# Bounding the queries by sums of squares on ScalarE, earlier, and one feed-forward due time set to nine units

## The chip, the cores and the metric

The kernel runs on one core of one Trainium2 chip. The metric is the device time of one execution in microseconds (us). Before the change three runs took 656.70, 658.43 and 662.99 us; their median is 658.43 us. The trace shown here is of a further, profiled execution that took 653.83 us, with a span of 652.1 us on the core.

## The reference, cut to what matters

There are 4 batches, 8 heads, 576 positions and a head size of 64, all in float32.

```
scores = q @ k.T / 8 + bias[h, i, j]        # bias: a small network of log1p|i - j| / log1p(max(i, 1))
attn   = exp(scores - max); attn = attn / (sum + 1e-9)
x      = attn @ v                           # laid out as (batch, position, 512)
out    = x + relu(layernorm(x) * g @ w1) @ w2     # w1: 512 x 2048, w2: 2048 x 512
```

The kernel multiplies on TensorE partly in float32 and partly in pairs of float16 numbers (a high part and a rest). For the pairs, q, k, v and the weights are first scaled by powers of two, so that no float16 overflows. To choose these powers it needs a bound on the size of q and k in each batch. How that bound of q is worked out is what changes.

## The kernel before, in words

**Units.** The attention is cut into 144 units (a batch, a chunk of 128 query positions, a head). A loop over steps u (0 to 158) writes the program out: at step u it writes the softmax of unit u, the second half of the softmax of unit u-1, the scores of later units, the product with v of unit u-3 or u-4, and whatever is filed under that step in a table of jobs (`at(step, fn)`). A scheduler then sets the order on each engine, by priority and by its own model of times; each engine and each DMA queue afterwards runs its list in order. Chunk 4 (the 64 last positions) and chunk 0 come first, in units 0 to 47, with their scores in float32; chunks 1 to 3 are units 48 to 143, with scores in float16 pairs. Units 0 to 23 turn their probabilities round on TensorE (L621, L622) and multiply them by v in float32 (L674); later units use float16 pairs (L627, L629) that a DMA transpose on SP's queue turns round (L635, tile `pt`).

**Softmax.** L598 on VectorE adds scores and bias and takes the minimum of each row; there is one for each unit, so the n-th L598 in time marks unit n-1. L603 on ScalarE takes the exponential.

**Bounds of q and k.** For units from 48 on, `q_load` (L443 to L449) loads all queries of a batch and chunk into a tile `qb` (two DMAs of 128 KB on SP's queue, L448, each made to wait for the newest L598), and `q_abs` takes its largest absolute value for each partition into a column of `kqa`, through `absmax` (L452, a reduce on VectorE, tied to the newest L598 as well). The tiles come from a pool of two buffers (`qhp`), so a load waits until the tile two loads earlier has been read. There are 12 such tiles: loads at steps 21 to 32, reductions at steps 25 to 36. At step 43 `kq_scale` (L462 to L485) adds up the partitions with a matmul (`kqps`, L464), takes maxima (L465, L467), scales them (L469) and, one step later (`fin`, through `defer`), makes the powers of two. `split_k` (L498, L501) and `split_q` (L513, L516) use them from step 44 on for the first units in float16 pairs; L531 are those units' scores.

**Weights.** `load_w` (L791) fetches 32 pieces of the feed-forward weights on SP's queue, `decode_w` (L807, L810, L812) unpacks them on VectorE, and `split_w` (L847 on ScalarE, L850 on VectorE) makes float16 pairs. A piece is loaded into a slot only when an earlier piece is decoded.

**Feed-forward.** A finished tile of 128 rows is normalised (`ln1`, `ln2`; L734, L735 on GpSimd, L761 and L764) and then needs 8 groups of matmuls: 4 times L873 (48 matmuls, into `hps`), each followed by L879 and L883 (relu and rest) and by L902 (12 matmuls, into `y`, added up by L913). With 18 tiles there are 144 groups. They are written between the units by a bank: at each step, what the tiles that are ready still need is divided by the steps until the next tile is due (`steps_av`), and whole groups are taken out. The due time is the tile's last unit plus 8 for last units below 26, plus 10 for those from 26 to 49, plus 9 after.

Of the kernel before, what the change touches and what calls it, by code (L numbers as in the profile page):

```python
# [14 lines left out]
AF = mybir.ActivationFunctionType  # L15
ALU = mybir.AluOpType
# [6 lines left out]
def kernel(  # L23
# [13 lines left out]
    V, S, G, T, SY = nc.vector, nc.scalar, nc.gpsimd, nc.tensor, nc.sync  # L37
# [43 lines left out]
    half4 = const.tile([128, 4], F32)  # L81
    gram = {}
    kqa = const.tile([128, 28], F32)
    kqs = const.tile([128, 8], F32)
# [27 lines left out]
    def pow2(am, s, inv):  # L112
        V.tensor_scalar(out=am, in0=am, scalar1=1e-30, scalar2=1e30, op0=ALU.max, op1=ALU.min)
        V.tensor_scalar(out=s.bitcast(I32), in0=am.bitcast(I32), scalar1=EXP_BITS,
                        scalar2=EXP_BITS, op0=ALU.bitwise_and, op1=ALU.bitwise_xor)
        if inv is not None:
            V.tensor_scalar(out=inv.bitcast(I32), in0=am.bitcast(I32), scalar1=EXP_BITS,
                            scalar2=None, op0=ALU.bitwise_and)
            V.tensor_scalar(out=inv, in0=inv, scalar1=0.5, scalar2=None, op0=ALU.mult)
# [26 lines left out]
    evi, ttri = {}, {}  # L146
    vpre = {}

    def after(ins, dep):
        if dep is not None:  # L150
            tc.add_manual_dep(ins.ins, dep.ins.name,
                              mybir.DependencyInfo(mybir.DependencyClass.Sync,
                                                   mybir.DependencyReason.DATA),
                              reason="pace")
# [230 lines left out]
    def defer(fn):  # L385
        later[1].append(fn)
# [38 lines left out]
    def k_gram(n):  # L425
        b = ORD[n][0]
        early = b < 2
        ps = (ps_h if early else ps_y).tile([128, 512], F32, tag="h" if early else "y1", name="kgram")
        ops = [(g, j) for g in range(4) for j in (0, 512, 128, 256, 384)]
        for x, (g, j) in enumerate(ops):  # L430
            w = min(128, 2 * HS - j)
            kb = kt[kuse[n], g].rearrange("p a b -> p (a b)").bitcast(BF16)
            blk = kb.rearrange("p (a b) -> p a b", b=2)[:, j:j + w, 1]
            m = T.matmul(out=ps[0:w, 0:w], lhsT=blk, rhs=blk, start=(x == 0), stop=(x == len(ops) - 1))
            if x == 0:
                after(m, ttri[max(ttri)])
        am = kqa[:, 4 * b:4 * b + 1]
        V.tensor_reduce(out=am, in_=ps[:, 0:128], op=ALU.max, axis=AX.X)
        G.tensor_tensor(out=am, in0=am, in1=half4[:, 0:1], op=ALU.pow)

    qld = {}

    def q_load(b, c):  # L443
        t = qhp.tile([128, 2, 4, 128], F16, tag="qh", name="qb")
        t = t.rearrange("p x a b -> p (x a b)").bitcast(F32)
        src = q_main[b, c, 0:64].rearrange("p (e h) q -> p e (h q)", e=2)
        for e in range(2):
            after(SY.dma_start(out=t[64 * e:64 * e + 64], in_=src[:, e]), ttri[max(ttri)])  # L448
        qld[b, c] = t  # L449

    def absmax(x, col):
        red = V.tensor_reduce(out=kqa[:, col:col + 1], in_=x, op=ALU.max, axis=AX.X,  # L452
                              apply_absolute_value=True)
        after(red, ttri[max(ttri)])

    def k_abs(n, g):
        absmax(kt[kuse[n], g].rearrange("p a b -> p (a b)"), 4 * ORD[n][0] + g)

    def q_abs(b, c):
        absmax(qld.pop((b, c)), 16 + 3 * b + c - 1)  # L460

    def kq_scale():  # L462
        ps = ps_y.tile([128, 512], F32, tag="y1", name="kqps")
        T.matmul(out=ps[:, 0:28], lhsT=one_sb, rhs=kqa, start=True, stop=True)  # L464
        V.tensor_reduce(out=kqs[:, 0:4], in_=ps[:, 0:16].rearrange("p (a b) -> p a b", b=4),  # L465
                        op=ALU.max, axis=AX.X)
        V.tensor_reduce(out=kqs[:, 4:8], in_=ps[:, 16:28].rearrange("p (a b) -> p a b", b=3),  # L467
                        op=ALU.max, axis=AX.X)
        V.tensor_scalar(out=kqs, in0=kqs, scalar1=2.0 ** -13, scalar2=None, op0=ALU.mult)  # L469

        def fin():
            pow2(kqs[:, 0:4], ksc, kinv)
            V.tensor_tensor(out=kqs[:, 4:8], in0=kqs[:, 4:8], in1=kinv, op=ALU.mult)
            V.tensor_reduce(out=pmx[:, 0:1], in_=kqs[:, 4:8], op=ALU.max, axis=AX.X)
            V.tensor_scalar(out=pmx[:, 0:1], in0=pmx[:, 0:1], scalar1=2.0 ** -40, scalar2=None,
                            op0=ALU.max)
            pow2(pmx[:, 0:1], pmx[:, 1:2], pmx[:, 2:3])
            V.tensor_scalar(out=qsc, in0=kinv, scalar1=pmx[:, 1:2], scalar2=None, op0=ALU.mult)
            V.tensor_scalar(out=ipf, in0=ip_sb[:, 16:32], scalar1=pmx[:, 1:2], scalar2=None,
                            op0=ALU.mult)  # L480
            V.tensor_scalar(out=cbf, in0=cb_sb, scalar1=pmx[:, 1:2], scalar2=None, op0=ALU.mult)
            V.tensor_scalar(out=pmx[:, 2:3], in0=pmx[:, 2:3], scalar1=-0.125, scalar2=None,
                            op0=ALU.mult)

        defer(fin)  # L485

    def scale_bias(h):
        raw = bt[seg[vis[ustart[2, 1]]], 1, h]
# [516 lines left out]
    def at(step, fn):  # L1005
        todo.setdefault(step, []).append(fn)
# [7 lines left out]
    for b in range(NB):  # L1014
        if b < 2:
            at((3, 10)[b], lambda b=b: k_gram(ORD.index((b, 0))))
        else:
            for g in range(4):
                at((39, 36)[b - 2] + g, lambda b=b, g=g: k_abs((7, 5)[b - 2], g))
        for c in (1, 2, 3):  # L1020
            at(24 + 3 * b + c - 4, lambda b=b, c=c: q_load(b, c))
            at(24 + 3 * b + c, lambda b=b, c=c: q_abs(b, c))
    at(43, kq_scale)
    for h in range(NH):
        at(ustart[2, 1] + h - 2, lambda h=h: scale_bias(h))
# [14 lines left out]
    NEARLY, LAG = 30, 3  # L1040
# [3 lines left out]
    steps_av = []  # L1044
    for b, c in tiles:
        last = ulast[b, c] if c < 4 else max(ulast[b, c], ulast[b + 1, c])
        steps_av.append(last + (4 + 2 + 3 - 1 if last < NEARLY - 4 else 10 if last < 50 else 9))
    u = 0
    while u < NU + 6 or jobs or cur_job or pend or yq:
        if u >= NEARLY:  # L1050
# [58 lines left out]
        for c in (1, 2, 3):  # L1109
            t = (u - cfirst[c] + 34) * 8 // 24 if c != 2 else (u - 50) * 8 // 20  # L1110
# [72 lines left out]
```

## Time and profile before

| what | value |
|---|---|
| runs | 656.70, 658.43, 662.99 us; median 658.43 us |
| profiled execution | 653.83 us, span 652.1 us |
| TensorE (PE) busy | 625.6 us, 96% |
| VectorE (DVE) busy | 519.8 us, 80% |
| ScalarE (ACT) busy | 423.4 us, 65% |
| GpSimd (POOL) busy | 57.5 us, 9% |
| granted TensorE clock | 0.996 of full speed |

Busy time is the time in which an engine executes something, and a span less a busy time is idle time. In the lists of single instructions each line gives the start and the duration in us, the engine, the line of the program, the operation, output and inputs, and how many instructions were merged; a bracket at the end is the idle time of the engine just before, with what ended it. Instructions of one engine overlap a little, so the cost of one in a full queue is the step from its start to the next start.

### The profile page before, as it was taken

What the parts mean: (1) busy time and instruction counts of PE and PEld (TensorE: products, weight loads), DVE (VectorE), ACT (ScalarE), POOL (GpSimd) and SP (SyncE); (2) the same over time, 40 slices, a digit from 0 to 9 for tenths busy, and PEclk for the clock granted to TensorE, in tenths of its full rate; (3) what the DMA queues carried; (4) which work ended last, traced back from release to release, by engine and by line L of the source; (5) the groups of instructions that cost most, each with busy time, mean ns of one, the idle gap of its engine ahead of it and who ended that gap; (6) DMA issues with size and microseconds to landing.
All of it is one profiled execution on the core that took longest, in us unless ns stands there. A gap on an engine that the chain in (4) does not pass through costs nothing. (4 is left out here: it accounts for less than half of the span.)

```text
span 652.1 us, 19876 instructions
## 1 busy us (share of the span) xinstructions
PE 625.6 (96%) x8163; PEld 442.1 (68%) x8163; DVE 519.8 (80%) x1182; ACT 423.4 (65%) x833; POOL 57.5 (9%) x98
## 2 busy tenths in 40 slices
PE   5799999998999999999999999999999999999997
PEld 4467767676566666666667666676777777777774
DVE  5698999799988888898978686988686888876421
ACT  5476785779956577998865676887555657654110
POOL 5331331000000000000000000001000000000000
PEclk9999999999999999999999999999999999999999
DMA  9899885774799996897977998887969979766100
GB/s 330 302 374 380 296 297 210 201 140 112 189 226 187 240 196 143 192 160 159 181 135 113 255 215 180 188 169 184 164 165 237 174 151 186 144 118 100 35 17 17
DMA packets 193675, 121.62 MB, mean 187 GB/s; under 512 B 164336, under 2 KB 164464, under 8 KB 193584
## 3 DMA queue, kind: packets, MB, share of 16 engines
q1 hardware_dynamic: 189200, 104.24, 70.6%
q0 software_dynamic: 4240, 15.93, 6.6%
q8 instruction: 64, 1.05, 0.7%
q10 hardware_dynamic: 144, 0.18, 0.2%
q14 instruction: 27, 0.22, 0.2%
HBM read 64.83 MB, written 15.63 MB: 123 GB/s over the span
## 5 line engine op out<-in xcount | busy, mean ns | idle before, releaser
L873 PE MATMUL hps<-xT,w 128*128 128x128 f16 x3240 | 195.0, 219 | 2.7 <-DVE hh L883 1.9
L873 PEld LDWEIGHTS <-w 128*128 128x128 f16 x3240 | 183.9, 98 | 9.6 <-issue 4.1
L902 PE MATMUL y<-w,hh 128*128 128x512 f16 x810 | 188.0, 379 | 0.6 <-ACT hh L879 0.5
L603 ACT ACTIVATE t<-t,m 128x576 f32<-128x576 f32 x144 | 110.8, 770 | 96.7 <-DVE m L598 96.4
L902 PEld LDWEIGHTS <-hh 128*128 128x128 f16 x864 | 79.9, 98 | 85.5 <-ACT wend L847 0.7
L627 DVE SCALAR_TENSOR_TENSOR e<-t,e 128x512 f16<-128x512 f32 x120 | 81.9, 683 | 20.6 <-ACT e L608 20.3
L879 ACT ACTIVATE hh<-hps 128x512 f16<-128x512 f32 x72 | 42.4, 588 | 70.4 <-PE hps L873 70.3
L883 DVE SCALAR_TENSOR_TENSOR hh<-hps,hh 128x512 f16<-128x512 f32 x72 | 49.4, 686 | 38.0 <-ACT hh L879 38.0
L608 ACT ACTIVATE e<-t 128x576 f16<-128x576 f32 x120 | 78.2, 672 | 0.8
L598 DVE CUSTOM_DVE_ANT_0 t<-sps,ldb,pmx 128x576 f32<-128x576 f32 x96 | 75.7, 810 | 3.7 <-PE sps L531 2.5
L645 PEld LDWEIGHTS <-pt 128*128 128x128 f16 (+1 forms) x1456 | 49.5, 100 | 25.9 <-issue 16.5
L645 PE MATMUL xps<-v,pt 128*128 128x64 f16 (+1 forms) x1456 | 58.6, 194 | 1.8 <-DMA pt<-e 1.2
L913 DVE SCALAR_TENSOR_TENSOR x<-y,ycs,x 128x512 f32<-128x512 f32 x58 | 43.1, 744 | 14.2 <-PE y L902 14.2
L734 POOL TENSOR_SCALAR rs<-mv 128x1 f32<-128x1 f32 x18 | 10.1, 562 | 478.7 <-DVE mv L733 225.6
L501 DVE SCALAR_TENSOR_TENSOR k<-kf,ksc,k 128x576 f16<-128x576 f32 x40 | 32.6, 815 | 16.7 <-ACT k L498 16.4
L531 PE MATMUL sps<-k,q 64*128 64x288 f16 x576 | 44.6, 284 | 1.0 <-DVE m L598 0.6
L598 DVE CUSTOM_DVE_ANT_0 t<-sps,ldb 128x576 f32<-128x576 f32 x48 | 35.9, 750 | 6.6 <-DMA ldb<-nb 3.6
L531 PEld LDWEIGHTS <-q 64*128 64x128 f16 x576 | 23.9, 94 | 16.2 <-issue 3.6
L555 PE MATMUL sps<-kf,qf 64*64 64x288 f32 (+1 forms) x256 | 34.4, 445 | 0.1
L498 ACT ACTIVATE k<-kf,ksc 128x576 f16<-128x576 f32 x40 | 30.4, 760 | 0.0
L175 ACT ACTIVATE r<-psi_sb,par_sb 128x416 f32<-128x416 f32 (+21 forms) x50 | 28.5, 612 | 2.9 <-DMA nb<-ev 1.8
L603 ACT ACTIVATION_READ_ACCUMULATOR t<-t,m 128x1 f32 x144 | 27.1, 188 | 0.0
(161 smaller groups left out, 785.9 us busy)
## 6 DMA issues: line engine op xcount, KB each, us to landing
kf<-in_k_s_dram SPq DMA_DIRECT2D x45, 288.0 KB, 3.4
ldb<-nb SPq DMA_DIRECT2D x40, 288.0 KB, 4.9
w<-in_w_ch_dram SPq DMA_DIRECT2D x22, 512.0 KB, 9.5
nb<-ev SPq DMA_DIRECT2D x24, 296.0 KB, 3.7
qf<-in_q_main_dram SPq DMA_DIRECT2D x24, 256.0 KB, 3.8
vf<-in_v_p_dram POOLq DMA_DIRECT2D x16, 320.0 KB, 7.3
kf<-in_k_s_dram POOLq DMA_DIRECT2D x15, 288.0 KB, 7.3
wend<-in_w_ch_dram SPq DMA_DIRECT2D x8, 512.0 KB, 4.8
```

The source lines that it names most:

```text
L531: m = T.matmul(out=ps[:, hf, 0:HS], lhsT=q[r, x, h % 4], rhs=kk[r, y, h % 2], start=(i == 0), stop=(i == 2), tile_position=(64 * hf, 0))
L555: m = T.matmul(out=o, lhsT=l, rhs=kk, start=True, stop=True, tile_position=(64 * hf, 64 * e))
L598: ttri[u] = V.tensor_tensor_reduce(out=halves(t), in0=ps[:, :, 0:HS], in1=halves(bias), scale=pmx[:, 2:3] if half(c) else -0.125, scalar=3e38,
L603: S.activation(t, t, AF.Exp, bias=m, scale=-1.0, accum_out=l8[b, c][:, h:h + 1])
L608: S.activation(e16[:, 0:SEQ], t, AF.Copy, scale=E_SCALE)
L627: V.scalar_tensor_tensor(out=e16[:, 640:1152], in0=t[:, 0:512], scalar=E_SCALE, in1=e16[:, 0:512], op0=ALU.mult, op1=ALU.subtract)
L645: T.matmul(out=o, lhsT=p[:, m], rhs=v[:, j, a, :], start=(i == 0), stop=(i == len(ops) - 1))
L873: T.matmul(out=h[:, idx * n:idx * n + n], lhsT=w[:, wo + kk * 128:wo + kk * 128 + 128], rhs=xT[k][:, xo + kk, 0:n], start=(i == 0), stop=( ...
L879: S.activation(hh[:, 0], h, AF.Relu)
L883: V.scalar_tensor_tensor(out=hh[:, 1], in0=h, scalar=0.0, in1=hh[:, 0], op0=ALU.max, op1=ALU.subtract)
L902: T.matmul(out=yps[k][t], lhsT=hh[:, a, o:o + 128], rhs=w[:, wo:wo + 512], start=(f == f0 and i == 0), stop=(f == f1 - 1 and i == 2))
L913: V.scalar_tensor_tensor(out=x, in0=y, scalar=ycs[:, g:g + 1], in1=x, op0=ALU.mult, op1=ALU.add)
```

## The change

The 12 maxima of `q_abs` become squares on ScalarE (`AF.Square`, in place, with the sum of each row as a second output); `kq_scale` takes the root of the largest sum (`ALU.pow` by a half on GpSimd) before the scaling, which moves into the deferred part. The loads and the squares are filed earlier: with n = 17 + (3b + c - 1) // 2, the loads at step n - 1 (16 to 21) and the squares at step n (17 to 22), two tiles a step. The due time of a tile whose last unit is 26 to 49 becomes its last unit plus 9.

```diff
     def q_abs(b, c):
-        absmax(qld.pop((b, c)), 16 + 3 * b + c - 1)
+        t, col = qld.pop((b, c)), 16 + 3 * b + c - 1
+        after(S.activation(t, t, AF.Square, accum_out=kqa[:, col:col + 1]), ttri[max(ttri)])
...
-        V.tensor_scalar(out=kqs, in0=kqs, scalar1=2.0 ** -13, scalar2=None, op0=ALU.mult)
+        G.tensor_tensor(out=kqs[:, 4:8], in0=kqs[:, 4:8], in1=half4, op=ALU.pow)
+
+        def fin1():
+            V.tensor_scalar(out=kqs, in0=kqs, scalar1=2.0 ** -13, scalar2=None, op0=ALU.mult)
+            fin()
...
-        defer(fin)
+        defer(fin1)
...
-            at(24 + 3 * b + c - 4, lambda b=b, c=c: q_load(b, c))
-            at(24 + 3 * b + c, lambda b=b, c=c: q_abs(b, c))
+            qn = 17 + (3 * b + c - 1) // 2
+            at(qn - 1, lambda b=b, c=c: q_load(b, c))
+            at(qn, lambda b=b, c=c: q_abs(b, c))
...
-        steps_av.append(last + (4 + 2 + 3 - 1 if last < NEARLY - 4 else 10 if last < 50 else 9))
+        steps_av.append(last + (4 + 2 + 3 - 1 if last < NEARLY - 4 else 9))
```

## Rows read from the trace of the kernel before

**Rows 1.** Busy time per stretch: PE, PEld, DVE, ACT, POOL, clock, DMA share, GB/s.
```profile
0.00:50.00 50.00, 38.45 (x528) 24.87 (x528) 36.20 (x96) 28.95 (x50) 20.34 (x37) 0.97 0.92 337
...
500.00:550.00 50.00, 50.00 (x713) 36.72 (x712) 42.72 (x94) 32.53 (x63) 2.25 (x4) 1.00 0.89 172
```

**Rows 2.** The chain that ended last, its last long piece: start, length, what.
```profile
642.72 5.19 PE y L902 x24
```

**Rows 3.** VectorE in order of time: the softmax of units 17, 20 and 35.
```profile
91.74 0.75 DVE L598 CUSTOM_DVE_ANT_0 t<-sps,ldb 128x576 f32<-128x576 f32 x1
...
99.23 0.75 DVE L598 CUSTOM_DVE_ANT_0 t<-sps,ldb 128x576 f32<-128x576 f32 x1
...
183.66 0.75 DVE L598 CUSTOM_DVE_ANT_0 t<-sps,ldb 128x576 f32<-128x576 f32 x1
```

**Rows 4.** Busy time per stretch, columns as in the first group.
```profile
86.00:127.00 41.00, 38.07 (x345) 29.09 (x344) 36.48 (x81) 27.09 (x60) 6.25 (x11) 1.00 0.72 235
...
134.00:192.00 58.00, 54.53 (x659) 37.91 (x657) 54.02 (x121) 46.29 (x89) 3.36 (x6) 1.00 0.75 168
192.00:220.00 28.00, 28.00 (x365) 18.49 (x362) 23.09 (x53) 16.54 (x33) 0.00 (x0) 1.00 1.00 199
220.00:260.00 40.00, 37.81 (x620) 26.46 (x614) 33.20 (x88) 28.75 (x55) 2.88 (x4) 1.00 0.87 195
```

**Rows 5.** Line L452: duration in ns (min/median/max), first and last start.
```profile
L452 DVE TENSOR_REDUCE kqa<-qb x12: 664/676/685, 134.8 to 190.7; 128x1 f32<-128x512 f32 x12
```

**Rows 6.** VectorE in order of time: one such reduction and the next instruction.
```profile
176.09 0.67 DVE L452 TENSOR_REDUCE kqa<-qb 128x1 f32<-128x512 f32 x1
176.69 0.74 DVE L598 CUSTOM_DVE_ANT_0 t<-sps,ldb 128x576 f32<-128x576 f32 x1
```

**Rows 7.** TensorE in order of time: the waits between 134 and 192 us.
```profile
151.38 2.39 PE L873 MATMUL hps<-xT,w 128*128 128x128 f16 x40 [0.73 <-DVE var L402]
...
157.51 0.58 PE L645 MATMUL xps<-v,pt 128*128 128x64 f16 x14 [1.23 <-DMA pt<-e]
...
174.92 0.83 PE L196 MATMUL bps<-r,nw_sb 128*32 128x368 f32 x8 [1.51 <-ACT r L175]
```

**Rows 8.** ScalarE in order of time: a pass with a sum of rows, and the next.
```profile
84.95 0.73 ACT L394 ACTIVATE vab<-vf 128x640 bf16<-128x640 f32 x1
...
85.67 1.07 ACT L205 ACTIVATE ev<-bps,cb_sb,par_sb 128x160 f32<-128x160 f32 x2
```

**Rows 9.** Busy time in steps of 10 us, columns as in the first group.
```profile
90.00:100.00 10.00, 9.21 (x85) 7.00 (x84) 10.00 (x28) 8.32 (x19) 2.62 (x5) 1.00 0.67 223
100.00:110.00 10.00, 9.01 (x91) 6.56 (x87) 9.64 (x17) 4.45 (x8) 1.13 (x3) 1.00 0.65 238
110.00:120.00 10.00, 9.65 (x98) 7.38 (x99) 9.43 (x21) 6.05 (x12) 1.97 (x3) 1.00 0.51 160
```

**Rows 10.** SP's queue in order of time: three weight loads.
```profile
98.15 14.37 SPq L791 DMA_DIRECT2D wend<-in_w_ch_dram  x3
```

**Rows 11.** DMA issues: output and input, queue, count, KB each, us to landing.
```profile
qb<-in_q_main_dram SPq DMA_DIRECT2D x24, 128.0 KB, 3.1
```

**Rows 12.** VectorE in order of time: its longest wait for a weight load.
```profile
125.21 0.43 DVE L807 TENSOR_SCALAR wend<-wend 128x512 uint32<-128x512 uint32 x1 [3.52 <-DMA wend<-in_w_ch_dram]
```

**Rows 13.** VectorE in order of time: the maximum and the scaling of the bounds.
```profile
222.02 0.16 DVE L467 TENSOR_REDUCE kqs<-kqps 128x4 f32<-128x12 f32 x1
...
223.74 0.15 DVE L469 TENSOR_SCALAR kqs<-kqs 128x8 f32<-128x8 f32 x1
```

**Rows 14.** GpSimd in order of time: a root of the same kind.
```profile
81.98 0.76 POOL L439 TENSOR_TENSOR kqa<-kqa,half 128x1 f32<-128x1 f32 x1
```

**Rows 15.** TensorE in order of time: the first scores in pairs, and a feed-forward group.
```profile
235.82 0.67 PE L531 MATMUL sps<-k,q 64*128 64x288 f16 x8 [0.37 <-DVE q L516]
...
253.45 2.84 PE L873 MATMUL hps<-xT,w 128*128 128x128 f16 x48 [1.00 <-DVE hh L883]
```

**Rows 16.** ScalarE's groups: count, busy us, mean ns, idle before: its only table load.
```profile
L175 ACT ACT_TABLE_LOAD x1 | 1.3, 1283 | 4.9 <-DMA par_sb<-in_par_dram 4.9
```

## The prediction

> **What bounds the kernel now.** I read the busy time by stretches first. From 500 to 550 us TensorE has no idle time at all, and the chain of waits, followed back from the end, ends in 5.19 us of feed-forward matmuls [rows 1, 2]. So the end is set by TensorE's work plus its idle time before that. The change takes no work from TensorE: its matmuls stay the same in kind and number. What it can win or lose is TensorE's idle time. Most of that lies in the first 50 us (11.55 us, [rows 1]), which the change doesn't touch: its first new instruction is filed under unit 16, near 90 us.
>
> Next I cut the stretches at the places that the change touches. The squares are filed at units 17 to 22, that is from 91.74 us on [rows 3]; the maxima that go lie between 134.8 and 191.3 us [rows 5]. TensorE's idle time is 41.00 - 38.07 = 2.93 us from 86 to 127 us, 58.00 - 54.53 = 3.47 us from 134 to 192, nothing from 192 to 220, and 2.19 us from 220 to 260 [rows 4]. Last I read what ended the 3.47 us: they are three waits of 0.73, 1.23 and 1.51 us [rows 7].
>
> **The parts, one by one.** A gain or loss stands with its sign; minus is faster.
>
> *The maxima leave VectorE.* One costs 0.60 us in a full queue, from its start to the next start [rows 6], so 12 free 7.2 us of an engine that is busy 54.02 of 58 us there [rows 4]. TensorE can get back no more than its idle time in that stretch. The waits of 0.73 us (for a small VectorE instruction) and of 1.23 us (for a transposing DMA whose input VectorE writes) end on VectorE's queue or behind it; four of the 12 maxima run ahead of the first (by the order of their starts), 2.4 us, more than both. The third, 1.51 us, is for a relu on ScalarE (L175), and it is what is late next; the change doesn't shorten it. I take -0.73 - 1.23 = **-2.0 us**; the ends are -3.5 (all three) and 0 (the waits are filled by the next one). The two loads of each tile also leave SP's queue here, where the same transposing DMAs stand behind them; that lies within the same ceiling.
>
> *The squares arrive on ScalarE.* The nearest row is the pass over v with a sum of rows, 640 columns against 512: 0.72 us from its start to the next [rows 8]. So 12 x 0.72 = 8.6 us at most, in a stretch where ScalarE has 41.00 - 27.09 = 13.9 us free [rows 4]. But the room isn't where the squares are filed. From 90 to 100 us ScalarE is idle 1.68 us, and units 17 to 20 all start in 91.74 to 99.23 us [rows 3, 9]: eight squares are 5.8 us, so 4.1 us don't fit and push exponentials behind them in ScalarE's order. From 100 to 120 us there are 9.5 us free [rows 9]. VectorE, busy 10.00, 9.64 and 9.43 of 10 us there, sets the pace with weight decoding that doesn't wait for ScalarE, so an exponential that comes late can be worked around. Ends: 0 and +4.1. I take **+0.7 us**, near the lower end, because VectorE is full and ScalarE isn't over the 30 us.
>
> *Loads.* The 24 DMAs of 128 KB, 3.1 MB [rows 11], move from after 114 us to steps 16 to 21. At 235 GB/s for a share of 0.72 [rows 4] the DMA engines would move 326 GB/s when full, so the loads need 9.6 us of the 41 x 0.28 = 11.5 us that are free: they fit, barely. On SP's queue they stand among the weight loads, three of which take 14.37 us from 98.15 us on, waiting for slots [rows 10]. Each pair of tiles must wait for the squares of the pair before (two buffers), and what stands behind it, later weight loads and the transposes of normalised tiles, waits too. Loads of k, q and v go by GpSimd's queue until unit 28 and aren't held up. The nearest row for such a delay is VectorE's wait of 3.52 us for a weight load [rows 12]. Ends: 0 and +3.5, one more such wait. I take **+0.3 us**: the same loads stood among the last weight loads before, so part of that wait is already paid.
>
> *The root.* The reduce ends at 222.18 us and the scaling starts at 223.74, with 1.56 us between that VectorE fills with other work [rows 13]. A root on GpSimd takes 0.76 us [rows 14], GpSimd is all but empty (2.88 us busy in 40, [rows 4]), and so the root fits between. Deferring the scaling by a step costs nothing that the following part didn't wait for already: `fin` was deferred by the same step. If the cover goes, the delay reaches TensorE's 0.37 us wait for the first split query [rows 15]. Ends 0 and +1.5 (twice the root, once for its wait in line); I take **+0.2 us**.
>
> *Nine units.* Going through the bank's arithmetic step by step with either due time, one group of matmuls moves: unit 35 gets two groups instead of one and unit 55 one instead of two, every other unit has its one, and from unit 55 on the two plans agree. In between each L873 and L902 comes a step earlier. Unit 35 starts at 183.66 us [rows 3] and TensorE has no gap from 192 to 220, so a group of 2.84 us (its length in [rows 15]) put there pushes all else back by as much, and unit 55 gives it back. What it can win is in the 2.19 us idle of 220 to 260 [rows 4], of which 1.00 us is a group that waits for the rest of the relu before it [rows 15]; the group written a step ahead changes that pairing. Ends: -2.2 and +1.0 (another such wait). I take **-0.7 us**.
>
> The sum is -2.0 + 0.7 + 0.3 + 0.2 - 0.7 = **-1.5 us**. Against the profiled execution's 653.83 us that is 652.3. The median of the three runs is 658.43, 4.6 us above it; I put the same change on the median: **656.9 us**.
>
> **A rule that speaks against it.** ScalarE loads its function tables once, for 1.28 us, ahead of the first relu, and then runs relu, identity, copy, absolute value and exponential to the end without another load [rows 16]. Square isn't among what this trace shows, so whether it needs another table is open here. The Trainium skill says (ScalarE: Activation LUTs, "Table sets: the hidden batching unit") that functions come in named sets, that a change of set costs a load, about 2.7 us with what goes with it, and that calls should be batched by set; it names relu, copy, identity and abs as members of every set, and not square. By the row the sum is as above; by that rule, with six pairs of squares and two changes for each, an estimate from that page's figure would add 12 x 2.7 = 32 us of ScalarE.
>
> **Rivals.**
> 1. *The stall moves* (18%). VectorE is freed, and TensorE then waits for ScalarE's relus of the bias, which already end the longest of the three waits [rows 7]. ScalarE is busy 46.29 of 58 us there [rows 4], which speaks for it. Then the first term is 0 and the rest +0.5: 658.9 us.
> 2. *All gaps close* (15%). The scheduler writes out new orders, and freed VectorE, emptier SP and the new phase of the groups close the idle time of all four stretches: 2.93 + 3.47 + 2.19 = 8.6 us, 649.8 us. Against it: 2.93 us of these lie where the change adds work.
> 3. *ScalarE's crowd and SP's queue decide* (13%): slower. In units 17 to 20 the squares wait for loads that wait behind weight loads, exponentials stand behind the squares, and the last weights come later. Price: +4.1 + 3.5 + 1.5 for the root, less the 2.0 us: +7.1, or 665.5 us. It decides when TensorE's idle time from 86 to 127 us grows from 2.93 to over 8 us. For it: TensorE is busy 9 of 10 us there [rows 9], so a delay has little to hide in. Against it: 9.5 us free on ScalarE just behind.
> 4. *Tables are swapped around the squares* (4%): slower. By the row's 1.28 us, 12 loads are 15.4 us; with the squares 24.0 us in 13.9 us of free time, 10.1 us over, less the 2.7 us of the first and last term: +7.4, or 665.8 us, and more if squares don't stand in pairs. For it: only that no square is in the trace. Against it: five other functions run from one load [rows 16].
>
> **How the numbers follow.** My own case has 50%: 656.9 us. Each is set on the median. One percent is 6.6 us, about what a measurement of this kernel can tell from no change (the three runs alone span 6.3 us): faster means under 651.8, slower over 665.0. My case and rival 1 lie within; rival 2 is faster; rivals 3 and 4 are slower, a few of them by less than 1%, as many as of my own case's upper bounds pass it. That gives 15% faster, 70% within, 15% slower. My terms' ends alone sum to -5.7 and +10.1. The range takes my case, rival 1 and the nearer parts of 2 and 3: 650 to 665 us; outside remain about half of rival 2, most of 3 and all of 4.
>
> **What would show it.** Twelve squares on ScalarE near 0.7 us each between 92 and 130 us, and one table load in all; no L452 on `qb`. TensorE's idle time from 134 to 192 us down from 3.47 to near 1.5, with the wait for L175 left; from 86 to 127 us still near 3 to 4 us. The root between the maxima and the scaling, and the first L531 no later against the units around it. Two feed-forward groups at unit 35, one at unit 55. Idle time from 86 to 134 us over 8 us, or ScalarE waiting for `qb` ahead of exponentials, would make the prediction wrong upward; gaps closing ahead of 127 us or after 220 us would make it wrong downward.

## The result, and the profile after

The changed kernel took 659.92 us (median of 21 runs, 656.36 to 666.31); the kernel before, run beside it, 655.2 us (21 runs, 652.52 to 662.99). The ratio is **1.0071, interval 1.0045 to 1.0098**: slower by 0.7%, or 4.7 us. The time lies in the predicted range and the change within 1%, but it goes the other way than the -1.5 us that I forecast. That 659.92 is close to 656.9 owes much to the base: the three runs that I set the forecast on had a median 3.2 us above that of the 21.

The profiled execution after has a span of 663.2 us against 652.1 and a mean granted clock of 0.980 against 0.996; it took 665.01 us, above its median, so its 11.1 us overstate the loss. What it shows is where such a loss is made. TensorE is busy 632.5 us against 625.6 with the same 8163 instructions: 6.9 of the 11.1 us are the same matmuls taking longer, and the other 4.2 are idle time. The mean granted clock of all 21 runs has a median of 0.988, against 0.994 in about 90 runs of the kernel before that stand beside the experiments.

Busy time per stretch after, same stretches and columns as [rows 4]:

```profile
86.00:127.00 41.00, 36.19 (x309) 25.99 (x309) 34.42 (x77) 29.07 (x71) 6.52 (x11) 0.92 0.82 252
134.00:192.00 58.00, 55.50 (x588) 40.20 (x589) 47.15 (x116) 47.67 (x95) 2.93 (x4) 0.91 0.52 106
192.00:220.00 28.00, 26.25 (x340) 18.44 (x339) 22.18 (x49) 16.63 (x32) 1.35 (x2) 1.00 0.97 204
220.00:260.00 40.00, 39.57 (x617) 27.67 (x615) 31.16 (x83) 21.93 (x41) 2.16 (x3) 1.00 0.82 173
```

Read the clock first: it was 1.00 in all four stretches before and is 0.92 and 0.91 in the first two. Then TensorE's idle time: 4.81 us against 2.93 from 86 to 127, 2.50 against 3.47 from 134 to 192, 1.75 against 0, and 0.43 against 2.19. Last the DMA share of the first stretch, 0.82 against 0.72, and VectorE there, 34.42 us against 36.48: it does less, not because it has less to do but because work reaches it later.

SP's queue after, in order of time (start, length, line, output and input, how many); the answer to [rows 10]:

```profile
96.20 2.84 SPq L448 DMA_DIRECT2D qb<-in_q_main_dram  x4
99.10 0.65 SPq L796 DMA_DIRECT2D wend<-in_w_ch_dram  x1
105.80 3.73 SPq L448 DMA_DIRECT2D qb<-in_q_main_dram  x4
109.58 0.58 SPq L796 DMA_DIRECT2D wend<-in_w_ch_dram  x1
112.81 6.37 SPq L448 DMA_DIRECT2D qb<-in_q_main_dram  x6
119.28 0.53 SPq L796 DMA_DIRECT2D wend<-in_w_ch_dram  x1
...
125.49 0.54 SPq L796 DMA_DIRECT2D wend<-in_w_ch_dram  x1
```

The three weight loads that had been issued at 98.15, 104.15 and 112.19 us now go out at 99.10, 109.58 and 119.28, between batches of query loads. Only the second is held by them for long. Each of the three needs a slot that a decoding sets free: before, each went out within 0.05 us of the end of a decoding (L812). After, the like decoding (L817) ends at 98.57, 105.89 and 119.17 us, so the second goes out 3.7 us late and the third at once. The first goes out nearly in time but takes longer to land. The time from issue to landing, of the load of `w` near 94 us and of this first one, before and then after:

```profile
w<-in_w_ch_dram SPq DMA_DIRECT2D x1, 512.0 KB, 5.4
DMA to landing us min/median/max: 6.3/6.3/6.3
```
```profile
w<-in_w_ch_dram SPq DMA_DIRECT2D x1, 512.0 KB, 8.3
DMA to landing us min/median/max: 12.4/12.4/12.4
```

VectorE's decoding follows, here with what ended its wait, the answer to [rows 12]:

```profile
103.00 0.43 DVE L812 TENSOR_SCALAR w<-w 128x512 uint32<-128x512 uint32 x1 [1.23 <-DMA w<-in_w_ch_dram]
111.62 0.43 DVE L812 TENSOR_SCALAR w<-wend 128x512 uint32<-128x512 uint32 x1 [1.22 <-DMA wend<-in_w_ch_dram]
116.75 0.42 DVE L812 TENSOR_SCALAR w<-wend 128x512 uint32<-128x512 uint32 x1
122.91 0.43 DVE L812 TENSOR_SCALAR wend<-wend 128x512 uint32<-128x512 uint32 x1 [0.34 <-DMA wend<-in_w_ch_dram]
130.98 0.43 DVE L812 TENSOR_SCALAR wend<-wend 128x512 uint32<-128x512 uint32 x1 [3.39 <-DMA wend<-in_w_ch_dram]
134.12 0.89 DVE L812 TENSOR_SCALAR wend<-wst 128x256 uint32<-128x256 uint32 x4
```

The same five steps of decoding before the last started at 99.91, 106.57, 108.00, 116.48 and 125.21 us, and the last at 128.35, of which three rows before:

```profile
99.91 0.42 DVE L807 TENSOR_SCALAR w<-w 128x512 uint32<-128x512 uint32 x1
106.57 0.41 DVE L807 TENSOR_SCALAR w<-wend 128x512 uint32<-128x512 uint32 x1
...
128.35 0.90 DVE L807 TENSOR_SCALAR wend<-wst 128x256 uint32<-128x256 uint32 x4
```

The weights are 3 to 9 us late and end 5.8 us late. The first two of these delays (103.00 and 111.62) belong to the two loads that were issued nearly in time and landed late, while the DMA share from 98 to 110 us was 0.95 against 0.71 before.

ScalarE after, in order of time, at the worst place:

```profile
105.05 0.63 ACT L461 ACTIVATE qb<-qb 128x512 f32<-128x512 f32 x1 [3.19 <-DMA qb<-in_q_main_dram]
...
107.69 0.63 ACT L461 ACTIVATE qb<-qb 128x512 f32<-128x512 f32 x1 [1.29 <-DMA qb<-in_q_main_dram]
108.22 0.19 ACT L461 ACTIVATION_READ_ACCUMULATOR qb<-qb 128x1 f32 x1
108.31 0.70 ACT L852 ACTIVATE w<-w,ws 128x512 f16<-128x512 f32 x1
108.92 0.57 ACT L884 ACTIVATE hh<-hps 128x512 f16<-128x512 f32 x1
```

TensorE in the same stretch, and matmuls of its next group of L907:

```profile
109.56 1.03 PE L907 MATMUL y<-w,hh 128*128 128x512 f16 x2 [3.20 <-ACT hh L884]
...
111.02 4.28 PE L907 MATMUL y<-w,hh 128*128 128x512 f16 x10
...
122.10 2.11 PE L907 MATMUL y<-w,hh 128*128 128x512 f16 x9
```

Busy time in two steps of 5 us, columns as in [rows 4]:

```profile
110.00:115.00 5.00, 5.00 (x17) 2.14 (x16) 2.79 (x5) 1.72 (x6) 0.00 (x0) 0.50 0.66 190
...
140.00:145.00 5.00, 5.00 (x39) 4.76 (x39) 2.02 (x6) 2.90 (x7) 0.90 (x1) 0.50 0.31 59
```

Read the three from top to bottom: a square stands 3.19 us and the next 1.29 us for its tile; a relu of the feed-forward (L884) stands behind them in ScalarE's order; TensorE waits 3.20 us for that relu; and then its matmuls run at half clock: ten of L907 take 4.28 us, where nine take 2.11 at 122.10. The last fence shows the granted clock as 0.50, the lower of its two levels (1.2 of 2.4 GHz), from 110 to 115 us and again from 140 to 145. Ahead of the second stretch, which begins near 135.5 us, TensorE had no long stall: from 130 us on its waits were 0.38 us (132.54) and 0.74 us (133.58, for a late weight).

### The profile page after: what moved, and what is told of

The parts are those of the page before. It is cut to its first block, busy times and chain, and to the rows that moved or that the text cites. A ratio compares the mean times of both kernels' runs of the same rounds, so it can differ in the third digit from the quotient of the medians.

```text
span 663.2 us, 19898 instructions
## 1 busy us (share of the span) xinstructions
PE 632.5 (95%) x8163; PEld 446.8 (67%) x8163; DVE 513.7 (77%) x1170; ACT 432.6 (65%) x857; POOL 59.7 (9%) x99
## 5 line engine op out<-in xcount | busy, mean ns | idle before, releaser
L878 PE MATMUL hps<-xT,w 128*128 128x128 f16 x3240 | 197.5, 220 | 2.4 <-DVE hh L888 1.9
L907 PE MATMUL y<-w,hh 128*128 128x512 f16 x810 | 190.2, 383 | 4.4 <-ACT hh L884 3.2
L878 PEld LDWEIGHTS <-w 128*128 128x128 f16 x3240 | 185.6, 98 | 11.6 <-issue 6.1
L907 PEld LDWEIGHTS <-hh 128*128 128x128 f16 x864 | 80.4, 99 | 90.2 <-ACT hh L884 3.4
L884 ACT ACTIVATE hh<-hps 128x512 f16<-128x512 f32 x72 | 42.4, 589 | 81.2 <-PE hps L878 81.0
L888 DVE SCALAR_TENSOR_TENSOR hh<-hps,hh 128x512 f16<-128x512 f32 x72 | 49.4, 686 | 47.9 <-ACT hh L884 47.8
L650 PEld LDWEIGHTS <-pt 128*128 128x128 f16 (+1 forms) x1456 | 49.2, 100 | 23.9 <-issue 13.1
L650 PE MATMUL xps<-v,pt 128*128 128x64 f16 (+1 forms) x1456 | 57.1, 194 | 2.1 <-DMA pt<-e 2.1
L536 PEld LDWEIGHTS <-q 64*128 64x128 f16 x576 | 23.9, 94 | 14.1 <-issue 1.8
```

The lines of the kernel that those rows point to most:

```text
L536: m = T.matmul(out=ps[:, hf, 0:HS], lhsT=q[r, x, h % 4], rhs=kk[r, y, h % 2], start=(i == 0), stop=(i == 2), tile_position=(64 * hf, 0))
L650: T.matmul(out=o, lhsT=p[:, m], rhs=v[:, j, a, :], start=(i == 0), stop=(i == len(ops) - 1))
L878: T.matmul(out=h[:, idx * n:idx * n + n], lhsT=w[:, wo + kk * 128:wo + kk * 128 + 128], rhs=xT[k][:, xo + kk, 0:n], start=(i == 0), stop=( ...
L884: S.activation(hh[:, 0], h, AF.Relu)
L888: V.scalar_tensor_tensor(out=hh[:, 1], in0=h, scalar=0.0, in1=hh[:, 0], op0=ALU.max, op1=ALU.subtract)
L907: T.matmul(out=yps[k][t], lhsT=hh[:, a, o:o + 128], rhs=w[:, wo:wo + 512], start=(f == f0 and i == 0), stop=(f == f1 - 1 and i == 2))
```

## The experiments

Three theories go through the expectations: W, ScalarE stands in order behind tiles that land late; S, the squares' own time is too much for ScalarE; D, the loads crowd out the weights, on the DMA engines and in SP's queue. N is the nine units. Edits are against the changed kernel unless "before" is said.

**Nine units alone** (before, with the new due time).

```diff
-        steps_av.append(... else 10 if last < 50 else 9))
+        steps_av.append(... else 9))
```


> Only the due time is changed (nine units), the maxima stay on VectorE at their old steps. Theory W (ScalarE stands in order behind late loads of the queries): no change that can be told, ratio 0.997 to 1.003. Rival N (the nine units cost the time): all of the loss, ratio near 1.007. Rival S (the squares are too much work for ScalarE): no change, as W.

1.0007 (0.9980 to 1.0035). The due time is worth nothing that can be measured, in either direction.

**All but the nine units** (ten put back).

```diff
-        steps_av.append(... else 9))
+        steps_av.append(... else 10 if last < 50 else 9))
```


> The changed kernel with the old due time (ten units). Theory W: the loss stays, ratio 1.005 to 1.010, and TensorE still waits about 3 us for the relu L884 near 106 us while ScalarE waits for qb. Rival N: the loss goes, ratio near 1.000. Rival S: the loss stays, as W.

1.0082 (1.0053 to 1.0112). The loss is with the squares and loads. TensorE waits for L884 twice, 2.3 us at the longest.

**Loads and squares at the old steps** (21 to 32 and 25 to 36), still on ScalarE, ten units.

```diff
-            at(qn - 1, lambda b=b, c=c: q_load(b, c))
-            at(qn, lambda b=b, c=c: q_abs(b, c))
+            at(24 + 3 * b + c - 4, lambda b=b, c=c: q_load(b, c))
+            at(24 + 3 * b + c, lambda b=b, c=c: q_abs(b, c))
```


> Squares on ScalarE and the root, but loads at steps 21 to 32 and squares at steps 25 to 36, as the maxima were, and the old due time. Theory W: the loads are there four steps ahead, ScalarE waits for none of them over 1 us, ratio 0.995 to 1.001. Rival S: ScalarE is 80% busy from 134 to 192 us and 8.6 us more make TensorE wait for its relus there: ratio 1.005 or more. Rival N: ratio near 1.000.

1.0083 (1.0058 to 1.0108): missed. The weights are in time here (the last decoding starts at 129.87 us), and a square stalls later: at 148.30 us ScalarE waits 3.08 us for a tile whose two loads, issued from 139.88 us on, took 6.6 and 7.7 us to land. In the kernel before, the query loads from 137 to 150 us took 3.4 us (median). What follows on TensorE:

```profile
152.44 0.30 PE L627 MATMUL ptl<-par_sb,t 128*64 128x128 f32 x1 [2.91 <-DVE hh L888]
...
154.23 5.30 PE L907 MATMUL y<-w,hh 128*128 128x512 f16 x12
```

A wait of 2.91 us, and then twelve matmuls of L907 in 5.30 us, where twelve take 2.75 us at a clock of 1.00 (at 157.38 us of the changed kernel).

**Maxima on VectorE at the new steps** (before, with loads and maxima at 16 to 21 and 17 to 22).

```diff
-            at(24 + 3 * b + c - 4, lambda b=b, c=c: q_load(b, c))
-            at(24 + 3 * b + c, lambda b=b, c=c: q_abs(b, c))
+            qn = 17 + (3 * b + c - 1) // 2
+            at(qn - 1, lambda b=b, c=c: q_load(b, c))
+            at(qn, lambda b=b, c=c: q_abs(b, c))
```


> Maxima on VectorE as before, but loads at steps 16 to 21 and maxima at 17 to 22, two a step, old due time. Theory W, which blames the early loads and not the engine: now VectorE stands behind the late loads, 3 us or more, and as VectorE is the full engine there the ratio is 1.005 to 1.015. Rival S (only ScalarE's work costs): ratio near 1.000, since the same work is only moved on VectorE. Rival N: 1.000.

1.0328 (1.0302 to 1.0355), the worst of all: the last decoding starts at 143.06 us. Of the three engines tried as readers, it hurts most on VectorE, which also decodes the weights.

**Squares of another tile** (the loads stay and nothing reads them; the squares read `gs_sb` and write to a scratch tile, so the queries are left out of the sums).

```diff
-        after(S.activation(t, t, AF.Square, accum_out=kqa[:, col:col + 1]), ttri[max(ttri)])
+        sq = e16p.tile([128, 1152], F16, tag="e16", name="sq").bitcast(BF16)[:, 0:512]
+        after(S.activation(sq, gs_sb, AF.Square, accum_out=kqa[:, col:col + 1]), ttri[max(ttri)])
```


> The changed kernel, but the 12 squares read a tile that has lain on chip since the start (the norm's weights), so they wait for no load; the 24 loads of the queries stay where they are and nothing reads them. It leaves the bound of the queries out. Theory W (ScalarE waits in order for late loads): the loss goes, ratio 0.993 to 1.001, TensorE's 3.2 us wait for the relu L884 is gone. Rival S (the squares themselves are too much for ScalarE near unit 20): the loss stays, ratio 1.005 or more. Rival D (the loads crowd out the weights on the DMA engines and SP's queue): the loss stays, as S.

1.0192 (1.0158 to 1.0225): W missed. ScalarE waits for no load, and the loss more than doubles. The last pieces are decoded from 137.45 to 141.54 us, and the list of waits from 86 to 134 us (who waits for whom, us in total, times, longest) names the weights:

```profile
PE gram L827 <- DVE w L818: 5.7, 2, 4.4
...
DVE w L813 <- DMA wend<-in_w_ch_dram: 4.7, 1, 4.7
```

**The same without the loads.**

```diff
...
-            after(SY.dma_start(out=t[64 * e:64 * e + 64], in_=src[:, e]), ttri[max(ttri)])
...
```


> As the run before it, but the 24 loads of the queries are left out too. It leaves the bound of the queries out. Theory W: the same as the run before, ratio 0.993 to 1.001. Rival S: 1.005 or more. Rival D: faster than the run before by 0.5% or more, VectorE's wait of 3.4 us for a weight load near 128 us gone.

1.0036 (1.0002 to 1.0070), the rival D's forecast. Squares alone cost 2.4 us (0.1 to 4.6). That is less than with loads that nobody reads (1.0192); against the squares of loaded tiles (1.0071 and 1.0082) the intervals overlap.

**Four buffers, loads two steps ahead.**

```diff
-        t = qhp.tile([128, 2, 4, 128], F16, tag="qh", name="qb")
+        t = e16p.tile([128, 1152], F16, tag="e16", name="qb").bitcast(F32)[:, 0:512]
...
-            at(qn - 1, lambda b=b, c=c: q_load(b, c))
+            at(qn - 2, lambda b=b, c=c: q_load(b, c))
```


> The changed kernel with the queries loaded two steps ahead instead of one, into a pool of four buffers instead of two (e16, hardly used before unit 24); squares where they were. Theory W: the waits of ScalarE for qb sink from 6.5 us to under 2 us in all and the ratio to 0.995 to 1.002. Rival D: the loads still stand among weight loads, and start in the crowded time before 100 us: ratio 1.005 or more. Rival S: 1.005 or more.

1.0145 (1.0123 to 1.0167). From 86 to 110 us the DMA share is 1.00, ScalarE still waits 6.5 us for tiles, and the last decoding starts at 138.34 us. More loads in flight make it worse, not better, which speaks for D.

**Squares at steps 31 to 42, loads two steps before,** ten units.

```diff
-            at(qn - 1, lambda b=b, c=c: q_load(b, c))
-            at(qn, lambda b=b, c=c: q_abs(b, c))
+            at(29 + n, lambda b=b, c=c: q_load(b, c))        # n = 3 * b + c - 1
+            at(31 + n, lambda b=b, c=c: q_abs(b, c))
```


> Squares on ScalarE one a step at steps 31 to 42, loads two steps ahead, two buffers, old due time. There TensorE has no idle time (192 to 220 us) and ScalarE is idle 11.5 of 28 us. Theory W: a wait for a load is covered by feed-forward groups already queued on TensorE; VectorE is freed from 134 us on: ratio 0.990 to 0.999. Rival S: ratio near 1.000, as ScalarE has room. Rival D: 1.000 to 1.005, since loads stand before the transposes on SP's queue.

1.0088 (1.0066 to 1.0109): missed. No weights are left to disturb, but ScalarE waits nine times for tiles (8.8 us), and a wait of TensorE for L888 at 204.12 us, 2.31 us long, is followed by 48 matmuls of L878 in 4.47 us against 2.84 [rows 15]. The loads themselves wait 1.0 us in all for a square to free a buffer, so the two buffers don't explain the late tiles here.

**What could be won at all** (before, without the loads and the maxima; the bounds are ones).

```diff
-            at(24 + 3 * b + c - 4, lambda b=b, c=c: q_load(b, c))
-            at(24 + 3 * b + c, lambda b=b, c=c: q_abs(b, c))
+    at(24, lambda: V.memset(kqa[:, 16:28], 1.0))
```


> The kernel before, without the 24 query loads and without the 12 maxima: the bounds of the queries are filled with ones, so this part of the computation is left out. It measures by itself what VectorE's relief and the loads can be worth at most. By my prediction's first term the gain is 2.0 us, at most 3.5 us of idle time from 134 to 192 us: ratio 0.995 to 0.998. If the two scores of waits in that stretch only change their releaser, 0.999 to 1.001. If the loads were the larger burden (they share the DMA engines with the transposes and, before 127 us, with the weights), 0.990 to 0.995, with idle time falling in 86 to 134 us as well as in 134 to 192 us.

1.0001 (0.9976 to 1.0026). Taking all of it away gains nothing that can be measured, 1.6 us at most. VectorE is busy 49.30 us from 134 to 192, against 54.02, and TensorE waits there as before, for the transposes:

```profile
159.86 0.58 PE L645 MATMUL xps<-v,pt 128*128 128x64 f16 x14 [1.25 <-DMA pt<-e]
177.36 0.68 PE L645 MATMUL xps<-v,pt 128*128 128x64 f16 x14 [2.15 <-DMA pt<-e]
```

**The root alone** (before, with the root on GpSimd and the scaling deferred).

```diff
-        V.tensor_scalar(out=kqs, in0=kqs, scalar1=2.0 ** -13, scalar2=None, op0=ALU.mult)
+        G.tensor_tensor(out=kqs[:, 4:8], in0=kqs[:, 4:8], in1=half4, op=ALU.pow)
...
-        defer(fin)
+        defer(fin1)
```


> The kernel before with the root on GpSimd and the deferred scaling alone (maxima stay, so the bound is the root of a maximum and not a bound: that part of the computation is changed). By my prediction's term +0.2 us: ratio 0.999 to 1.002, and the first scores in pairs start where they did against their unit. If the chain from the bounds to the first split query is tight, +1.5 us or more: 1.002 to 1.005.

0.9995 (0.9973 to 1.0016): nothing.

**The loads from GpSimd's queue,** once with the squares at steps 31 to 42, once at the new steps; ten units both.

```diff
-            after(SY.dma_start(out=t[64 * e:64 * e + 64], in_=src[:, e]), ttri[max(ttri)])
+            after(G.dma_start(out=t[64 * e:64 * e + 64], in_=src[:, e]), ttri[max(ttri)])
```


> The squares at steps 31 to 42 as in the run before (1.0088), ten units for the feed-forward, but the 24 loads issued from GpSimd's queue and not SP's. If the loss there came from SP's queue (transposes and query loads behind one another, the two-buffer wait holding up what stands behind it), it goes: 0.992 to 1.000, and the waits of ScalarE for the query tile fall below 3 us in all. If it comes from ScalarE standing in order behind a tile that two buffers deliver late, or from the DMA engines, whatever the queue, it stays: 1.005 to 1.010.

> The squares and loads at the changed kernel's steps (17 to 22 and 16 to 21), ten units, the 24 loads issued from GpSimd's queue. The same without that edit was 1.0082. If SP's queue makes the loads late (they stand among weight loads that wait for slots), ScalarE's waits for the query tile shrink and the ratio is 0.998 to 1.003; weights then come no later than before. If the DMA engines are what is short from 90 to 112 us, the tiles land as late or the weights do: 1.006 to 1.012.

1.0118 (1.0076 to 1.0159), not told apart from the 1.0088 by SP's queue, and 1.0294 (1.0258 to 1.0329), far worse than 1.0082. In the second, GpSimd's queue waits 23.9 us for squares to set buffers free, and it also issues the loads of k, q and v, which stand behind. The weights now share their queue with no query load, and still the last pieces are decoded from 133.60 to 137.83 us, against 128.35 before. So their lateness doesn't need SP's order.

**Squares of 8 columns.** All 512 are loaded; the sums leave out the rest.

```diff
-        after(S.activation(t, t, AF.Square, accum_out=kqa[:, col:col + 1]), ttri[max(ttri)])
+        after(S.activation(t[:, 0:8], t[:, 0:8], AF.Square, accum_out=kqa[:, col:col + 1]),
+              ttri[max(ttri)])
```


> The changed kernel with ten units (1.0082 in full), its squares cut to 8 of 512 columns (the other columns are left out of the sums): loads, order and waits stay, ScalarE's own work for the squares shrinks. If ScalarE standing in order behind late tiles (W), or the loads on the DMA engines (D), make the loss, it stays: 1.006 to 1.010, and ScalarE still waits about 6 us for the query tile. If the squares' own time on ScalarE (S) makes it, it goes: 0.998 to 1.003.

1.0126 (1.0081 to 1.0171): S isn't needed. Loads and waits with hardly any of the squares' time lose as much.

**The tile read on GpSimd,** by a product of one column, once beside squares of another tile on ScalarE, once alone (there it writes to `kqa`).

```diff
+        after(G.tensor_tensor(out=t[:, 0:1], in0=t[:, 0:1], in1=t[:, 0:1], op=ALU.mult),
+              ttri[max(ttri)])
```


> The loads at the changed kernel's steps, each tile read and set free by a one-column product on GpSimd; ScalarE makes its 12 squares of full length, but of a resident tile (the queries are left out of the sums), so it never waits for a load while the loads keep the pace that two buffers and their reader give. Ten units. W: the loss goes, 1.000 to 1.004, as in the run without loads (1.0036). D: it stays, 1.006 to 1.010, with TensorE or VectorE waiting for weights instead. S: it stays too.

> The loads at the changed kernel's steps, read by the one-column product on GpSimd alone; no squares, no maxima (the bounds are left out but for one column). Ten units. W and S: no loss, 0.998 to 1.002, like the kernel without loads and maxima (1.0001). D: the loss that belongs to the loads shows by itself, 1.004 to 1.008.

1.0238 (1.0213 to 1.0263) and 1.0134 (1.0097 to 1.0170). Without a single square, and with ScalarE free of waits, the loss is there. But GpSimd waited 20.8 us for tiles in the second, so a reader in order wasn't excluded.

**Loads that nobody reads,** early and at their old steps; no squares, no maxima.

```diff
-            at(qn, lambda b=b, c=c: q_abs(b, c))
...
+    at(24, lambda: V.memset(kqa[:, 16:28], 1.0))
```


> The loads at the changed kernel's steps and nothing that reads them; no squares, no maxima (the bounds of the queries are filled with ones and left out). Ten units. No engine stands behind a load, so what it costs against the kernel without loads and maxima (1.0001) belongs to the loads alone, on the DMA engines and on SP's queue. D: 1.006 to 1.015. W: no loss, 0.998 to 1.003.

> The kernel before with its loads at their old steps (21 to 32) and nothing that reads them; no maxima (the bounds are filled with ones and left out). If the place of the loads, among the last weight loads, is what makes their price, 0.998 to 1.002 here. If loads cost wherever they stand once no reader paces them, 1.005 or more, as in the early place.

Early **1.0116** (1.0073 to 1.0158), as D had it: loads alone, moved early, lose no less than the whole change. At the old steps **1.0030** (1.0006 to 1.0053), between the two forecasts. Busy time from 86 to 134 us and the last decoding, of the early loads and then of those at the old place:

```profile
86.00:134.00 48.00, 41.96 (x347) 31.62 (x345) 37.36 (x81) 27.49 (x64) 6.62 (x11) 0.93 0.82 247
...
134.16 0.90 DVE L812 TENSOR_SCALAR wend<-wst 128x256 uint32<-128x256 uint32 x4
```
```profile
86.00:134.00 48.00, 44.46 (x395) 34.01 (x396) 42.74 (x101) 32.58 (x74) 6.23 (x11) 1.00 0.67 218
...
129.33 0.90 DVE L807 TENSOR_SCALAR wend<-wst 128x256 uint32<-128x256 uint32 x4
```

TensorE is idle 6.04 us against 3.54 and its clock is 0.93 against 1.00; the weights end 4.8 us later. SP's queue of the early loads where the delay begins:

```profile
97.44 0.34 SPq L796 DMA_DIRECT2D wend<-in_w_ch_dram  x1
104.04 3.57 SPq L448 DMA_DIRECT2D qb<-in_q_main_dram  x4
107.66 0.58 SPq L796 DMA_DIRECT2D wend<-in_w_ch_dram  x1
```

Two things make the weights late. The load of 97.44 us lands 12.9 us after its issue, against 6.1 us for its like with the loads at the old steps (99.18 us). And the query load of 104.04 us has waited 6.2 us, until an earlier one into its buffer had landed; the weight load of 107.66 us goes out behind it, 1.9 us after the decoding that frees its slot (105.80).

**Loads of a quarter of the size,** as many as before, with squares of a quarter.

```diff
-            after(SY.dma_start(out=t[64 * e:64 * e + 64], in_=src[:, e]), ttri[max(ttri)])
+            after(SY.dma_start(out=t[64 * e:64 * e + 64, 0:128], in_=src[:, e, 0:128]), ttri[max(ttri)])
```


> The changed kernel's order and steps with ten units, each of the 24 loads and 12 squares cut to a quarter (128 of 512 columns; the rest is left out of the sums): as many DMAs and waits, 0.8 MB instead of 3.1. If the amount that the DMA engines move decides, the loss goes (0.998 to 1.003), and the weights land as they did before. If SP's queue, with its number of DMAs and its waits in order, or ScalarE's order decides, it stays (1.006 to 1.012).

1.0096 (1.0059 to 1.0133): the loss stays, but the late weights go. They are 2.4 us late in the middle (118.84 us for the step at 116.48) and 0.6 us at the end (128.91 us). No weight load is held by query loads any more: 105.77 and 114.42 us are within 0.1 us of the decodings that free their slots. The table has us from issue to landing for two weight loads, and the DMA share, in one profile of each kernel (the quarter loads compare with the changed kernel with ten units):

| | before | changed | changed, ten units | early, no reader | a quarter | old steps, no reader |
|---|---|---|---|---|---|---|
| load of `w` near 94 us | 5.4 | 8.3 | 7.3 | 8.7 | 5.6 | 5.8 |
| load of `wend` near 98 us | 6.3 | 12.4 | 10.9 | 12.9 | 7.2 | 6.1 |
| DMA share, 98 to 110 us | 0.71 | 0.95 | 1.01 | 0.98 | 0.76 | 0.78 |

So in these profiles the lateness of the weights goes with the amount of data, and late weights aren't the only way to lose 1%: here ScalarE waits 8.5 us for query tiles instead. In its profile 9.4 of 9.7 us are TensorE's busy time, so the clock is nearly all of the loss:

```profile
122.00:128.00 6.00, 4.45 (x34) 3.25 (x33) 3.79 (x8) 4.12 (x10) 0.00 (x0) 1.00 1.01 264
128.00:134.00 6.00, 5.46 (x26) 4.96 (x27) 4.52 (x14) 2.97 (x11) 0.00 (x0) 0.50 0.09 31
134.00:140.00 6.00, 6.00 (x28) 4.79 (x27) 2.51 (x10) 3.39 (x9) 0.00 (x0) 0.50 0.17 49
```

Here 1.55 us of idle time from 122 to 128, in waits of at most 1.18 us, were followed by 12 us and more at half clock.

## Why the prediction was wrong

**What bounds the kernel: right.** The last matmuls are the same 5.19 us of L907, and the loss is made of idle time and of slow matmuls ahead of it. Idle time also moves: from 192 to 220 us 1.75 us opened and from 220 to 260 us 1.76 us closed.

**The maxima, -2.0 us: wrong, no gain.** Without loads and maxima the kernel is 0.1 us slower (-1.6 to +1.7 us), and without the maxima alone, the loads left at their old steps, 2.0 us slower (0.4 to 3.5). I had put the waits for the transposes "behind VectorE's queue" because VectorE writes their input. With 12 maxima fewer those waits are still there, 1.25 and 2.15 us long: rival 1's form, a stall that moves, though to the transposes and not to the relus. Seeing that a busy engine feeds a transfer doesn't show that the transfer waits for it.

**The squares, +0.7 us: not contradicted.** A square takes 626 ns, with 188 ns for the sum overlapping it, near the 0.72 us from the row of the pass over v. Alone they cost 2.4 us (0.1 to 4.6; my ends were 0 and 4.1). The trace after has the one table load of [rows 16] and no other. The Trainium skill (ScalarE: Activation LUTs, "Table sets: the hidden batching unit"), read as I did, would have put an estimate of 32 us here; by the measurement square needed no set of its own in this kernel.

**The loads, +0.3 us of 0 to +3.5: the step that failed.** Early loads that nothing reads cost 7.6 us by themselves (4.8 to 10.3, from 1.0116 of 655 us), more than my upper end; at their old steps they cost 2.0 us (0.4 to 3.5), and with the maxima as their readers nothing that can be told. I had asked whether their bytes fit into the free share of the DMA engines from 86 to 127 us ("they fit, barely"). That average hid the place: from 98 to 110 us the share was 0.71 already, and with the loads it is 0.95. There other transfers take longer (the load of `wend` 12.4 us for 6.3), the weights end 5 to 6 us late (134.16 and 134.12 us for 128.35), and TensorE's idle time from 86 to 134 us is 6.0 us against 3.5 with the same loads at their old steps. The order on SP's queue, where I did look, adds to it: a query load that waits for its buffer holds one weight load for 1.9 us, and 3.7 us in the changed kernel. I discounted that wait, since "the same loads stood among the last weight loads before"; there they stood behind the three that matter. The late weights aren't all: with a quarter of the bytes they are nearly in time and the loss is as large. What the rows show there is ScalarE waiting for tiles, 8.5 us in all; in the changed kernel it is 6.5 us. That this wait makes the loss there is argued, not shown.

**The price of a stall: missing.** No term of mine held the clock. In the profiled pair the same matmuls take 6.9 of the 11.1 us more, which is more than all idle time. Over all runs the fall of the mean clock from 0.994 to 0.988 makes an estimate of 4 us (0.6% of 655, with TensorE busy throughout), nearly the whole 4.7. The clock also differs from run to run of one kernel (0.984 to 1.000 before), so the split in one profile is that execution's. Each of my upper ends for a wait of 2 to 3 us was too low by what the matmuls behind it lose at half clock.

**The root, +0.2 us, and the nine units, -0.7 us.** The root alone is 0.9995 (-1.8 to +1.0 us). It took 1.02 us on GpSimd, not 0.76, and the scaling still started 1.33 us after the maximum's end, against 1.56. Nine units are +0.5 us (-1.3 to +2.3): the idle time that they could close from 220 to 260 us did close, to 0.43 us in the changed kernel's profile and to 0.42 us with nine units alone, where none opened from 192 to 220, and still no gain in time can be told.

**Rival 3 had much of the mechanism,** ScalarE waiting for its tiles and weights that come late, at 13%; that the weights' own transfers would slow down wasn't in it. Its price was 7.1 us where 4.7 was measured. Its condition, over 8 us of idle time from 86 to 127, was not met (4.81 us), and yet it decided, because more than half of the loss in the profiled pair is in the clock and not in idle time. The loads and the squares don't add: loads alone 1.0116, squares alone 1.0036, both 1.0082; the intervals of the first and the last overlap, so whether the squares' pacing helps is open.

**What stays open.** How much of the 4.7 us is late weights and how much ScalarE standing in order behind tiles: every early kernel had the one or both. Idle time and clock from 86 to 134 us don't settle it, since the squares without loads have 5.3 us of idle time and a clock of 0.93 there in their profile and lose 0.4%. Why the quarter loads lose is seen only as clock. That late squares lose too (1.0083, 1.0088) isn't explained: the tiles come late there as well, but neither by the weights nor, in the second, by the two buffers. Early loads spread out in time, or put behind the weight loads, weren't tried. No version ran faster than the kernel before.

## What to carry to other kernels

Before pricing a moved load, read the DMA share and the landing times of the very stretch that it moves into, not an average over 41 us; then list what its queue issues behind it and what each entry waits for. Bound what a change can win by a run or a row in which the work is simply gone; here it was nothing, and only losses were left. Where TensorE is full to the end, read the granted clock beside the idle time: a stall can cost its own length and as much again in the matmuls behind it.

## What the runs showed of the hardware that was not expected

- A stall of 2.3 to 3.2 us on TensorE was followed by several us at half clock in three kernels (rows at 109.56 and 152.44 us, and at 204.12 us of the squares at steps 31 to 42); in the quarter loads the clock fell behind waits of at most 1.18 us, and at 135.5 us of the changed kernel behind waits of at most 0.74. The kernel before had waits of 1.34 us (110.35 us) and 1.51 us [rows 7] at a clock of 1.00. The length of one wait doesn't tell the two apart.
- Early loads took longer and so did their neighbours: from 86 to 134 us the time from issue to landing went from 5.4 to 8.3 us for the load of `w`, and from 5.2 to 8.0 us for `vf`, which goes by GpSimd's queue, at a DMA share of 0.95 from 98 to 110 us. One load of `wend` took 12.4 us against 6.3.
- The same root took 0.76 us on one column [rows 14] and 1.02 us on four.
